# Long-convolution block with a two-layer perceptron: fixed engine order, transposing loads, and product tiles of two frequencies

## The chip, the cores and the metric

One core of one Trainium2 chip. The metric is device time in microseconds, median of several runs, lower is better. A ratio is the mean time of one kernel's fast runs over the mean of the other's fast runs of the same rounds on the same chip, so it is not quite the ratio of the two medians that are quoted beside it. The experiments ran on three chips, and the kernel before ran beside each of them (medians 287.61, 289.42 and 287.06 us): where two experiments from different chips are compared, the ratios count.

## The reference

```
x = q                                      # 2048 tokens x 512 channels, bf16
k_shift[t] = sum over j of 0..3 of shift_k[j] * k[t-j]
kv = k_shift * v
y  = irfft(rfft(kv, 4096) * rfft(ssm_k, 4096))[:2048] + kv * ssm_D      # per channel, float32
h  = x + layernorm(x) * y
out = h + relu(layernorm(h) @ w1) @ w2     # w1: 512 x 1376
```

PE is the matrix engine and PSUM the buffer that its results land in; a piece of it of 512 floats in each partition is called a bank here (pools `psF` and `psI` of the changed kernel hold eight tiles of that size). A copy out of PSUM is called an eviction. PE is called cold where its granted clock is 0.50 and warm where it is 1.00: in the kernel before, matmuls of 256 columns start 213 ns apart from 64 to 69 us, at 0.50, and 118 ns apart from 72 to 80 us, at 1.00.

Both kernels do the transforms as matrix products in two steps (64 points by 64), the filter's first and then the signal's, multiply the two spectra (the "product"), go back in two steps, and end with layer norms and the dense layers. The product stage: for each frequency column k1 PE makes the real and the imaginary part of the signal's spectrum `u` in PSUM, VectorE and GpSimd multiply them with the filter's spectrum `kf`, PE adds the four partial products into `psy`, and ScalarE copies the sum over `kf`.

## The kernel before

The parts that the change and the argument touch:

```python
# _stage2: one k1 at a time, one PSUM tile (one bank) holding both halves
for k1 in range(32):
    ps = psum.tile([P, 2, 256], F32, tag="ps", name="ps2")
    nc.tensor.matmul(out=ps[:, 0, :], lhsT=cc[:, k1, :], rhs=a_in[:, k1, :], start=True, stop=False)
    ...                                                       # four matmuls in all
    consume(k1, ps)

# product of the spectra; psum bufs=5
nc.scalar.copy(out=usb[:], in_=u[:, :, NV:DC, :])
nc.vector.tensor_tensor(out=t12v[:, :, 0:NV, :], in0=u[:, :, 0:NV, :], in1=k_same[:, :, 0:NV, :], op=ALU.mult)
nc.vector.tensor_tensor(out=t34v[:, :, 0:NV, :], in0=u[:, :, 0:NV, :], in1=k_swap(0, NV), op=ALU.mult)
... # GpSimd the last quarter of each
def finish(k1, t12, t34):
    psy = psum.tile([P, 2, DC * 64], F32, tag="psy", name="psy", bufs=3)
    ...                                                       # four matmuls, then
    nc.scalar.copy(out=kf[:, :, k1, :, :].rearrange("p r g s -> p s r g"), in_=psy[:].rearrange(...))

# first inverse: statistics of the layer norm ahead of it in VectorE's order; weights of stride 512 bytes
for t in range(NT):
    nc.vector.bn_stats(out=st1[:, t, :], in_=xh[:, t, :])
    nc.vector.bn_aggr(out=mv1[:, t, :], in_=st1[:, t, :])
for g in range(64):
    nc.tensor.matmul(out=pso, lhsT=kf[:, :, :, g, 0], rhs=dre[:], start=True, stop=False)
    nc.tensor.matmul(out=pso, lhsT=kf[:, :, :, g, 1], rhs=dim[:], start=False, stop=True)
    ...
# tail: groups of the second inverse stand between the dense layers
inv2_group(0); inv2_group(1); mlp1(0); inv2_group(2); mlp1(1); ...
```

The order of each engine's instructions was left to the scheduler.

## Time and profile before

288.3 us (median of 4 runs, 287.98 to 289.86). By stage, from busy times in stretches of the span:

| stage | us |
|---|---|
| head: tables, transposed filter | 42.5 |
| filter: first and second transform | 17.0 and 18.3 |
| signal: layout, first transform | 4.5 and 14.0 |
| product | 35.6 |
| first inverse | 36.1 |
| tail: second inverse, layer norms, dense layers | 119.4 |

The stretches themselves, the waits and the chain stand in the prediction. Two groups of the product stage are added here. The columns are line, engine, operation, output and input, shapes, count, then busy us and mean ns of one, then the idle time before it and what ended it:

```profile
L348 ACT CAST kf<-psy 128x512 fp32r<-128x512 f32 x32 | 20.1, 631 | 3.6 <-POOL t L336 1.4
L334 DVE TENSOR_TENSOR t<-ps,kf 128x384 fp32r<-128x384 f32 x32 | 17.6, 550 | 1.9 <-ACT usb L333 1.7
```

The idle time of ScalarE and VectorE ahead of these instructions is a few us of 35.6.

### The profile page before, as it was taken

To read this page: it belongs to the slowest core of one execution; us is meant where nothing else is said; L and a number is where in the kernel's file an instruction comes from. 1 tells how busy PE (TensorE), PEld (TensorE's weight loads), DVE (VectorE), ACT (ScalarE), POOL (GpSimd) and SP (SyncE) were. 2 spreads that over 40 slices of the span, in tenths; PEclk is the share of its full clock that TensorE was granted. 3 is DMA by queue.
4 is the path that set the end of the run, shared out by engine and by line. 5 is a ranking of instruction groups with operands and counts; after the bars stand their busy time and mean duration, and the time that the engine had idled before them with its cause. 6 is when DMAs were issued, how large, how long until landed. Compare 5 with 4: busy or idle time off the path is not lost.

```text
span 287.4 us, 7594 instructions
## 1 busy us (share of the span) xinstructions
PE 225.3 (78%) x3098; PEld 156.9 (55%) x3108; DVE 196.2 (68%) x449; ACT 152.9 (53%) x327; POOL 48.0 (17%) x97
## 2 busy tenths in 40 slices
PE   2027007889986699988999385999999998999994
PEld 0027005529975699977999273544544554444441
DVE  4899999985896599996836936578294258233221
ACT  1039999998885278877966313464352045113000
POOL 9921000000000389983000000000000000000000
PEclk9999555556995599996899757589999999999999
DMA  5699400000000000029156000000000200020122
GB/s 120 150 344 229 98 0 6 5 2 0 2 3 5 2 2 2 2 66 208 22 183 211 0 2 5 2 2 1 5 0 5 57 18 0 18 57 0 38 56 55
DMA packets 7876, 14.25 MB, mean 50 GB/s; under 512 B 2210, under 2 KB 5634, under 8 KB 7714
## 3 DMA queue, kind: packets, MB, share of 16 engines
q1 hardware_dynamic: 4898, 11.31, 15.5%
q10 hardware_dynamic: 2944, 2.46, 3.0%
q8 instruction: 24, 0.39, 0.6%
q14 instruction: 10, 0.08, 0.1%
HBM read 11.67 MB, written 2.10 MB: 48 GB/s over the span
## 4 chain that ended last, share of the span: by engine, by line
PE 60%; ACT 11%; DVE 9%; issue 3%; DMA 2%; ACTq 0%; DVEq 0%; SPq 0%
PE ps2m L465 12%; PE ps1m L454 12%; PE pz L422 7%; ACT a1k L270 5%; PE psi L391 4%; PE psi L392 4%; DVE st L382 3%; PE ps L112 3%; PE ps L114 3%; PE ps L115 3%; PE ps L113 3%; PE pt L444 1%; DMA xh<-in_A_q_dram 1%; ACT xfl L283 1%; DVE a1x L304 1%
## 5 line engine op out<-in xcount | busy, mean ns | idle before, releaser
L454 PE MATMUL ps1m<-hlnT,w 128*128 128x512 bf16 (+1 forms) x169 | 41.6, 387 | 2.1 <-ACT h1T L457 1.0
L465 PE MATMUL ps2m<-w,h1T 128*128 128x512 bf16 (+1 forms) x173 | 38.4, 379 | 0.2
L468 DVE TENSOR_TENSOR o<-ps2m,xh 128x512 bf16<-128x512 f32 x16 | 11.1, 692 | 29.6 <-PE ps2m L465 17.8
L391 PE MATMUL psi<-dre,kf 128*128 128x256 f32 x64 | 26.4, 412 | 5.3 <-DVE bp L396 3.1
L454 PEld LDWEIGHTS <-w 128*128 128x128 bf16 (+1 forms) x176 | 17.0, 102 | 23.2 <-issue 7.8
L457 ACT ACTIVATE h1T<-ps1m 128x512 bf16<-128x512 f32 (+1 forms) x24 | 14.4, 599 | 27.4 <-PE ps1m L454 24.7
L465 PEld LDWEIGHTS <-h1T 128*128 128x128 bf16 (+1 forms) x176 | 17.2, 98 | 20.8
L422 PE MATMUL pz<-bp,ecore 32*32 32x128 f32 x1024 | 25.2, 393 | 3.5 <-ACT zt L428 2.1
L336 POOL TENSOR_TENSOR t<-usb,kf 128x128 fp32r<-128x128 f32 x32 | 15.1, 473 | 73.3 <-ACT usb L333 71.6
L392 PE MATMUL psi<-dim,kf 128*128 128x256 f32 x64 | 25.4, 397 | 0.0
L99 PE MATMUL ps<-f_hi,kfl 32*128 32x64 bf16 x256 | 10.3, 234 | 18.5 <-ACT kfl L230 15.7
L391 PEld LDWEIGHTS psi<-dre,kf 128*128 128x128 f32 x64 | 20.0, 313 | 7.1 <-DVE bp L396 3.4
L394 ACT COPY bp<-psi 128x256 f32<-128x256 f32 x48 | 17.8, 372 | 9.3 <-PE psi L392 7.6
L428 ACT CAST zt<-pz 128x512 bf16<-128x512 f32 x16 | 8.2, 600 | 26.4 <-PE pz L422 26.4
L348 ACT CAST kf<-psy 128x512 fp32r<-128x512 f32 x32 | 20.1, 631 | 3.6 <-POOL t L336 1.4
L422 PEld LDWEIGHTS pz<-bp,ecore 32*32 32x32 f32 x1024 | 15.5, 117 | 10.4 <-issue 4.1
L392 PEld LDWEIGHTS psi<-dim,kf 128*128 128x128 f32 x64 | 20.3, 317 | 0.0
L433 DVE TENSOR_TENSOR gt<-zt,qln 128x512 bf16<-128x512 bf16 x16 | 6.5, 407 | 19.8 <-ACT zt L428 19.8
L334 DVE TENSOR_TENSOR t<-ps,kf 128x384 fp32r<-128x384 f32 x32 | 17.6, 550 | 1.9 <-ACT usb L333 1.7
L459 DVE TENSOR_SCALAR h1T<-ps1m 128x512 bf16<-128x512 f32 x20 | 13.6, 682 | 7.1 <-PE ps1m L454 7.1
L229 PE MATMUL pst<-ident,sk 128*128 128x128 bf16 x64 | 6.7, 299 | 14.0 <-DMA sk<-in_A_ssm_k_dram 14.0
L335 DVE TENSOR_TENSOR t<-ps,kf 128x384 fp32r<-128x384 f32 x32 | 17.5, 548 | 0.0
(133 smaller groups left out, 575.7 us busy)
## 6 DMA issues: line engine op xcount, KB each, us to landing
vt<-in_A_v_dram SPq DMA_DIRECT2D x16, 128.0 KB, 8.4
sk<-in_A_ssm_k_dram SPq DMA_DIRECT2D x1, 2048.0 KB
xh<-in_A_q_dram SPq DMA_DIRECT2D x4, 512.0 KB, 8.4
kh<-in_A_k_dram SPq DMA_DIRECT2D x13, 128.0 KB, 4.5
w<-in_B_w_dram SPq DMA_DIRECT2D x1, 1376.0 KB, 6.4
w<-in_B_w_dram ACTq DMA_DIRECT2D x1, 1280.0 KB, 9.6
out_dram<-o SPq DMA_DIRECT2D x32, 32.0 KB, 1.5
out_dram<-o ACTq DMA_DIRECT2D x32, 32.0 KB, 1.7
```

Of the source, the lines that this page charges most:

```text
L270: _stage1(nc, psum, kfl, f1hi, f1lo, a1k, lambda i, d, s: nc.scalar.copy(out=d, in_=s))
L334: nc.vector.tensor_tensor(out=t12v[:, :, 0:NV, :], in0=u[:, :, 0:NV, :], in1=k_same[:, :, 0:NV, :], op=ALU.mult)
L335: nc.vector.tensor_tensor(out=t34v[:, :, 0:NV, :], in0=u[:, :, 0:NV, :], in1=k_swap(0, NV), op=ALU.mult)
L336: nc.gpsimd.tensor_tensor(out=t12v[:, :, NV:DC, :], in0=usb[:], in1=k_same[:, :, NV:DC, :], op=ALU.mult)
L348: nc.scalar.copy(out=kf[:, :, k1, :, :].rearrange("p r g s -> p s r g"), in_=psy[:].rearrange("p s (r g) -> p s r g", r=DC))
L391: nc.tensor.matmul(out=pso, lhsT=kf[:, :, :, g, 0], rhs=dre[:], start=True, stop=False)
L392: nc.tensor.matmul(out=pso, lhsT=kf[:, :, :, g, 1], rhs=dim[:], start=False, stop=True)
L394: nc.scalar.copy(out=bp[:, g, :, :, :], in_=ps[:])
L422: nc.tensor.matmul(out=pz[32 * a:32 * a + 32, rg, l4, :], lhsT=ecore[rows, rho, n2, :], rhs=rhs, start=(rho == 0), stop=(rho == 1), tile_p ...
L454: nc.tensor.matmul(out=ps1[:fsz, :], lhsT=w1[:, c, fc * P:fc * P + fsz], rhs=hlnT[:, c, sc * SCW:(sc + 1) * SCW], start=(c == 0), stop=(c ...
L457: nc.scalar.activation(out=h1T[:fsz, fc, sc * SCW:(sc + 1) * SCW], in_=ps1[:fsz, :], func=ACT.Relu)
L465: nc.tensor.matmul(out=ps2[:], lhsT=h1T[:ksz, fc, t * P:(t + 1) * P], rhs=w2[:ksz, fc, :], start=(fc == 0), stop=(fc == NFC - 1))
```

## The change

Its intent: shorten the head (the shift product leaves VectorE and becomes 64 matmuls with diagonal matrices, on k and v brought in transposed by DMA; tables with fewer instructions), halve the evictions of the second transform and the multiplications of the product by taking two k1 in a tile (ScalarE keeps its 64 instructions in the product), store the product so that the first inverse loads contiguous weights, and fix the order of every engine by hand. The diff, cut to its core:

```diff
+    ctx.enter_context(tc.manual_schedule())
+    nc.sync.dma_start_transpose(out=vT[:, :, CH * c:CH * c + CH], in_=v_d[CH * c:CH * c + CH, :])
-    ... (the shift product on VectorE, 64 instructions)
+            for j in range(KS):
+                nc.tensor.matmul(out=ps[:], lhsT=wdiag[:, rg, j, :], rhs=kcs[c][:, rg, 16 - j:CH + 16 - j],
+                                 start=(j == 0), stop=(j == KS - 1))
-    psum = pl.push("psP", bufs=5, space=PSUM)
+    psum = pl.push("psP", bufs=2, space=PSUM)
+    NJ = 176
+    LAG = 2
+    def product(kp):
+        u = psum.tile([P, 2, 2, 256], F32, tag="u", name="u")
+        for s in range(2):
+            stage2(u[:, s, :, :], a1x, kp, s)
+            uj = u[:, s, :, :].rearrange("p k j -> p j k")
+            nc.scalar.copy(out=usb[:, s, :, :], in_=uj[:, po, :])
+            t = prod.tile([P, 2, 256, 2], F32R, tag=f"t{s}", name=f"t{s}")
+            ... (VectorE multiplies 176 of 256 columns from PSUM, GpSimd 80 from usb)
+    def finish():
+        psy = psum.tile([P, 2, 512], F32, tag="psy", name="psy")
+        for s, (a, b, m) in enumerate(((tr[:, 0], ti[:, 1], ineg), (tr[:, 1], ti[:, 0], ipos))):
+            for m_, t_, first in ((ipos, a, True), (m, b, False)):
+                nc.tensor.matmul(out=psy[:, s, :], lhsT=m_[:], rhs=t_.rearrange("p j k -> p (j k)"),
+                                 start=first, stop=not first)
+            nc.scalar.copy(out=kf[:, s, :, 2 * kp:2 * kp + 2], in_=psy[:, s, :].rearrange("p (j k) -> p j k", k=2))
-        nc.tensor.matmul(out=pso, lhsT=kf[:, :, :, g, 0], rhs=dre[:], start=True, stop=False)
+                nc.tensor.matmul(out=ps[:, i, :], lhsT=kf[:, c, 4 * m:4 * m + 4, :].rearrange("p r k -> p (r k)"),
+                                 rhs=d[:].rearrange("p a b -> p (a b)"), start=(c == 0), stop=(c == 1))
-    inv2_group(0)
-    inv2_group(1)
-    mlp1(0)
-    inv2_group(2)
-    ...
+    for q in range(4):
+        inv2(q)
+    gate(0, qs[0])
+    h = hln_(0)
+    transposes(0, h)
+    ...
```

A half of `u` (s = 0 or 1) is 512 floats and has a PSUM bank to itself.

## The prediction

> **What bounds the kernel now.** I read the page's forty slices first, then the chain that ended last, then cut the span where that chain changes subject and asked for busy time in each stretch. The columns are start:end, length, busy us of PE, weight loads, VectorE, ScalarE, GpSimd, granted clock, DMA share, GB/s.
>
> ```profile
> PEclk9999555556995599996899757589999999999999
> ```
>
> That row is the clock granted to PE in tenths: 5 from slice 4 to 8 (29 to 65 us), in slices 12 and 13, 23 and 25, always where PE waits for others. The stretches:
>
> ```profile
> 0.00:28.00 28.00, 8.70 (x68) 7.04 (x68) 22.68 (x58) 9.79 (x18) 16.27 (x25) 1.00 0.80 211
> 28.00:42.50 14.50, 0.00 (x0) 0.00 (x0) 14.50 (x28) 14.40 (x20) 0.00 (x0) 0.52 0.27 59
> 42.50:59.50 17.00, 13.86 (x535) 9.10 (x536) 16.96 (x30) 15.76 (x34) 0.00 (x0) 0.50 0.02 4
> 59.50:64.00 4.50, 3.20 (x46) 0.78 (x40) 3.84 (x7) 4.50 (x12) 0.00 (x0) 0.50 0.01 4
> 64.00:82.30 18.30, 18.30 (x192) 18.10 (x179) 13.46 (x32) 15.16 (x38) 0.00 (x0) 0.84 0.00 1
> 82.30:96.30 14.00, 8.24 (x485) 6.35 (x474) 10.07 (x17) 8.64 (x18) 0.00 (x0) 0.66 0.02 4
> 96.30:131.90 35.60, 33.59 (x257) 32.44 (x257) 33.64 (x72) 26.80 (x64) 30.56 (x70) 0.93 0.14 30
> 131.90:154.00 22.10, 22.07 (x97) 21.78 (x98) 10.75 (x26) 17.43 (x44) 1.19 (x2) 0.86 0.57 161
> 154.00:168.00 14.00, 9.00 (x33) 7.42 (x32) 12.55 (x39) 6.10 (x15) 0.00 (x0) 0.78 0.09 28
> 168.00:187.00 19.00, 14.90 (x529) 9.69 (x531) 9.48 (x31) 5.79 (x13) 0.00 (x0) 0.59 0.02 3
> 187.00:287.40 100.40, 93.46 (x902) 44.21 (x910) 48.27 (x117) 28.56 (x60) 0.00 (x0) 0.99 0.09 22
> ```
>
> No single engine bounds it; nine stages follow each other, each with its own limit. (1) 0 to 42.5: tables and the transposed filter. PE has nothing to do from 28 to 42.5, while VectorE (14.50 of 14.50) and ScalarE (14.40) are full. (2) 42.5 to 59.5, the filter's first transform: ScalarE, 15.76 of 17, alone carries 32 evictions at 0.49 us. (3) 59.5 to 64, layout of the signal. (4) 64 to 82.3, second transform: PE full. (5) 82.3 to 96.3, the signal's first transform: evictions on two engines, clock 0.66. (6) 96.3 to 131.9, product: PE 33.59 and VectorE 33.64 of 35.6. (7) 131.9 to 168, first inverse step: PE with slow weight loads, then a hole. (8) 168 to 187.4, second inverse and layer norms, and (9) the two dense layers, PE 93.46 of 100.4 from 187 on.
>
> Two waits name the head and the chain names the hole:
>
> ```profile
> PE ps L99 <- ACT kfl L230: 15.7, 1, 15.7
> ACT f_f L67 <- DVE f_aph L60: 15.9, 1, 15.9
> ```
> ```profile
> 154.45 1.27 DVE st L382 x2
> 155.81 0.58 DVE st L382
> ```
>
> The first transform waited 15.7 us for the filter copies on ScalarE, and that engine's sine work had itself waited 15.9 us for phase arithmetic on VectorE, which was queued among the shift products. At 154 the chain runs through sixteen layer-norm statistics on VectorE: they sit in front of an eviction that PE needs.
>
> [...]
>
> ```profile
> L391 PE MATMUL psi<-dre,kf 128*128 128x256 f32 x64 | 26.4, 412 | 5.3 <-DVE bp L396 3.1 <-ACT bp L394 1.4 <-ACT kf L348 0.8
> L391 PEld LDWEIGHTS psi<-dre,kf 128*128 128x128 f32 x64 | 20.0, 313 | 7.1 <-DVE bp L396 3.4 <-ACT bp L394 2.7 <-ACT kf L348 1.0
> L113 PEld LDWEIGHTS ps<-a1x,c2s 128*128 128x128 f32 x32 | 6.6, 207 | 0.0
> L345 PEld LDWEIGHTS psy<-t,ineg 128*128 128x128 f32 x32 | 6.1, 192 | 0.0
> ```
>
> The inverse's stationary tile has a 512-byte stride and loads in 313 ns, so its matmuls start 225 ns apart at full clock; contiguous tiles load in 192 to 207 ns (cold ones included) and start 118 apart. [...] In the changed program's built order [...] each of its 16 blocks waits for the eviction of the block before, though that lies in other columns. [...]
>
> **The change part by part**, as estimates from rows above and from single durations in the groups by shape.
>
> Head. Removed: the 64 instructions of the shift product on VectorE (8 chunks of 8, about 0.6 us each, 40 us), the cos/sin phase pairs, the quarter-size sine calls, three 3.5 us table clears. The filter load goes first: here it took 8.8 us from issue to use, so it is there at about 9.5. 64 transposes took 6.74 us: PE ends at 16.2. ScalarE: sine over 32 elements took 229 ns and over 512 took 633, so 0.84 ns an element; four of 2048 cost 7.7 us, starting when VectorE's turns are done (two of about 1.25 us after a 2 us GpSimd iota, so about 7), so to 14.7; then three copies of 1.03. Five more go to VectorE. The copies end at about 18 instead of 42.5.
>
> First transforms. 32 evictions split evenly: VectorE 16 x 0.62 = 9.9, plus a first batch of 0.9 and issue gaps: the signal's stage already does this and took 14.0, with 3 us of PE gaps. Four row groups now alternate before the second weight comes, so I take 12.5 each (were 17.0 and 14.0).
>
> Second transform of the filter: 128 matmuls x 118 ns = 15.1, plus a cold start of some 3: 18 (was 18.3). Evictions, half as many and twice as wide, stay under it.
>
> Signal side. The shift product was hidden on VectorE in the head; now it is 64 diagonal matmuls x 216 ns (the dense layers' spacing) = 13.8 plus a last multiply of 1: 15. Chunks 2 and 3 of k reuse the buffer of the filter's transform, so their load is issued only when that ends; PE has 6.9 us of chunks 0 and 1 meanwhile[...]. Then 64 transposes 6.8 plus the last copy 1.2: 8. Together 23 where 4.5 stood.
>
> Product: PE 16 x (8 x 118 ns + 4 x 225) = 29.5; ScalarE 16 x 2 x (0.29 + 0.63) = 29; VectorE 32 x (550 ns + 320 x 1.04 - 90 of overlap) = 25; GpSimd 32 parts of 320 elements: 128 take 0.42 us start to start, so between 0.8 and 1.05, 26 to 34. VectorE is relieved, the others not: with fill and drain 35 (was 35.6).
>
> First inverse: 128 x 118 ns = 15.1; ScalarE 20 x 0.53 + 8 x 0.6 = 15.4; VectorE 12 x 0.64 + 16 x 0.42 = 14.4. All even: 17 (was 36.1). The statistics leave this stage.
>
> To here 18 + 12.5 + 18 + 15 + 8 + 12.5 + 35 + 17 = 136, against 168: 32 gained.
>
> Tail (was 119.4). The fourth group of 256 second-inverse records ran 228.1 to 232.5, 17.3 ns each at full clock; the first ran 23 ns each, half cold. A block is 64 records: 1.1 to 1.5, plus 0.35 for the last one's own duration, 0.6 for the ScalarE copy, 0.1 between: 2.1 to 2.5, and 16 strictly in turn are 34 to 40: 36. Before, groups 3 and 4 took 5.0 and 4.4 beside other work. After the last copy: square root 0.3, reciprocal 0.2, normalise 0.4, four rounds of transposes and copy through one PSUM buffer at 1.3: 6. Dense layers 352 x 216 ns = 76, cold start 2. The three later transpose groups stand in line in front of matmuls, 4 x (0.4 + 0.65) less the last: 11. Two square roots stand in ScalarE's queue ahead of the relus and wait for statistics: 2 x 2 = 4. End: last sum 0.7, four stores issued and landed 3.3: 4. Sum 36 + 6 + 76 + 2 + 11 + 4 + 4 = 139, so 20 lost.
>
> 136 + 139 = **275 us**, 13 less than before.
>
> **Rivals.** (a) The tail loses nothing: if block waits were hidden and the transposes short, the tail would stay near 119 and the time about 255. For it: one fixed order saves end-of-kernel store waits (11.8 us of waits for stores, mostly slack). Against: the waits stand in the built order. (b) The tail eats all: the half-idle second inverse keeps PE cold (stage 5 cooled to 0.50 under such a duty), 40 us for it, and cold dense matmuls after each transposes round; with 4 more in each of the two first transforms, 290. (c) A transfer becomes the bound: [...] 5 to 10 us on the path, 283. (d) GpSimd, at 8-byte runs 128 bytes apart, [...] 42 us of product, 282.
>
> **Range and chances.** The head and the first inverse are worth some 43 us and rest on measured rows; the conv stage costs 18 with little doubt. The tail is the weak term, 125 to 148, and loads and GpSimd can only add. 258 to 291 should hold it. Below 282.6 counts as over 2% faster: 0.72. Within 2%: 0.21. Slower: 0.07.
>
> **What would show it right or wrong.** Right: first matmul of the first transform near 18; weight loads of the first inverse near 190 ns and its stage 16 to 18; no statistics in front of its evictions; 16 waits of the second inverse for its ScalarE copy, about 0.7 each; PE idle on the transposes' copy in three places. Wrong: a wait on the k transposing loads, a product over 39, or a second inverse of 20 us, which would make the whole about 258.

What was cut from the prediction, at the marks, came from elsewhere or was assumed, and no trace of this case shows it: rules on the clock, on memory access and on waits in PSUM, the rate of transposing loads and what was concluded from it, the rate that rival (c) assumed and the time of an instruction that rival (d) assumed. The sentence on the 16 blocks speaks of the second inverse; that the loads of k would be hidden behind 6.9 us of work is an assumption (in the run no matmul waited for them). Three figures of the product's term come from the kernel before: 1.04 ns an element is the slope between VectorE's 425 ns for 256 elements and 692 for 512, the 90 ns are two instructions of 550 ns that start 460 apart, and 216 ns is the spacing of the dense layers' matmuls of 512 columns. The 225 ns for 512 columns in the product were an estimate and no row of that trace; the kernel with both tiles split later gave 230.

## The result

347.97 us (median of 4 runs, 346.56 to 348.56) against 288.28: ratio 1.2056, 95% interval 1.201 to 1.210. **Slower by 21%**, where 275 us were predicted. The result is correct in value.

The clock row of the forty slices, which answers to the first line that the prediction shows:

```profile
PEclk9955899985555555555555995555589999999999
```

In slices 10 to 21 (counted from 0), that is from about 87 to 187 us, PE never leaves half clock. The stretches of the changed kernel (same columns as in the prediction: start:end, length, busy us of PE, weight loads, VectorE, ScalarE, GpSimd, then clock, DMA share, GB/s):

```profile
0.00:18.10 18.10, 6.63 (x64) 6.50 (x64) 16.11 (x31) 12.83 (x10) 10.29 (x18) 0.98 0.99 231
18.10:33.10 15.00, 9.13 (x512) 7.73 (x512) 9.66 (x18) 8.51 (x17) 11.63 (x16) 0.50 0.46 81
...
51.00:65.70 14.70, 13.88 (x64) 6.14 (x64) 11.43 (x17) 0.60 (x1) 0.00 (x0) 1.00 0.48 75
65.70:73.10 7.40, 5.97 (x66) 5.87 (x67) 4.91 (x5) 4.06 (x4) 0.00 (x0) 1.00 0.00 0
73.10:87.20 14.10, 8.67 (x513) 7.24 (x513) 9.94 (x16) 8.21 (x16) 0.79 (x2) 0.58 0.02 5
87.20:187.30 100.10, 66.79 (x192) 46.95 (x192) 28.49 (x32) 28.57 (x64) 28.71 (x36) 0.50 0.00 0
187.30:205.60 18.30, 17.36 (x128) 17.16 (x128) 16.09 (x31) 15.22 (x29) 2.85 (x5) 0.89 0.98 268
205.60:241.00 35.40, 24.29 (x1024) 15.04 (x1024) 9.16 (x28) 10.44 (x18) 0.00 (x0) 0.54 0.02 5
```

| stage | before | predicted | measured |
|---|---|---|---|
| head | 42.5 | 18 | 18.1 |
| filter, first transform | 17.0 | 12.5 | 15.0 |
| filter, second transform | 18.3 | 18 | 17.9 |
| signal: diagonal matmuls; transposes | 4.5 | 15; 8 | 14.7; 7.4 |
| signal, first transform | 14.0 | 12.5 | 14.1 |
| **product** | 35.6 | **35** | **100.1** |
| first inverse, to the first block of the second | 36.1 | 17 | 18.3 |
| tail | 119.4 | 139 | 139.2 |

One stage carries the miss: 65 of the 73 us. In it PE, VectorE, ScalarE and GpSimd are busy 66.8, 28.5, 28.6 and 28.7 of 100.1 us, and the 66.8 are at half clock. Apart from PE's, the single instructions have about the sizes that were predicted (VectorE 892 ns where the prediction's sum gives 793, GpSimd 886, ScalarE 292 and 601), so none of them is slow; they stand one after another. The waits say what for (us in total, times, longest):

```profile
PE u L232 <- DVE t L322: 21.7, 16, 1.4
PE psy L332 <- ACT kf L334: 10.9, 16, 0.7
```

One wait of each kind in each of the 16 pairs. The timeline shows a full pair, from 139.96 to 146.16 us; columns are start, length, engine, instruction, count, and in brackets the idle time before it and its releaser (only some lines are copied):

```profile
139.96 0.58 PE L232 MATMUL u<-a1x,c2n 128*128 128x256 f32 x1 [1.36 <-DVE t L322]
...
142.08 0.60 ACT L334 CAST kf<-psy 128x512 fp32r<-128x512 f32 x1 [0.56 <-PE psy L332]
142.73 1.22 PE L332 MATMUL psy<-t,ipos 128*128 128x512 f32 x2 [0.69 <-ACT kf L334]
143.75 0.41 PE L232 MATMUL u<-a1x,c2c 128*128 128x256 f32 x1
...
144.89 0.29 ACT L318 COPY usb<-u 128x160 f32<-128x160 f32 x1 [0.30 <-PE u L234]
145.22 0.89 DVE L322 TENSOR_TENSOR t<-u,kf 128x704 fp32r<-128x704 f32 x1 [2.71 <-ACT usb L318]
...
146.16 0.58 PE L232 MATMUL u<-a1x,c2n 128*128 128x256 f32 x1 [1.36 <-DVE t L322]
```

PE writes the first half of `u` (143.75), ScalarE copies its part (144.89), VectorE multiplies (145.22), and only then PE starts the second half (146.16), which needs none of that. The same happens in `psy`: its second half waits for the copy of the first. 16 x 6.20 us = 99.2. By the trace, which infers releasers from semaphore events, these two matmuls wait for a reader of the other half. The reading that the experiments test is that dependencies are kept by PSUM tile, and both halves belong to one tile. In the timeline no later matmul starts inside the gaps of 0.69 and 1.36 us, so whatever was ready behind such a wait stood too.

### The profile page after: what moved, and what is told of

Read it like the earlier page. It is cut to its first block, busy times and chain, and to the rows that moved or that the text cites. A ratio compares the mean times of both kernels' runs of the same rounds, so it can differ in the third digit from the quotient of the medians.

```text
span 344.8 us, 7155 instructions
## 1 busy us (share of the span) xinstructions
PE 254.9 (74%) x3094; PEld 169.8 (49%) x3104; DVE 163.0 (47%) x313; ACT 135.0 (39%) x240; POOL 54.3 (16%) x75
## 4 chain that ended last, share of the span: by engine, by line
PE 66%; ACT 10%; DVE 10%; issue 3%; ACTq 0%; DVEq 0%
PE ps2m L495 11%; PE ps1m L482 10%; PE psy L332 10%; PE pz L420 7%; PE u L232 6%; PE psi L393 5%; DVE t L322 5%; PE pkv L282 4%; PE u L234 4%; ACT kf L334 3%; ACT zt L423 3%; PE ps2k L232 3%; PE ps2k L234 2%; ACT hlnT L470 2%; DVE st L433 2%
## 5 line engine op out<-in xcount | busy, mean ns | idle before, releaser
L322 DVE TENSOR_TENSOR t<-u,kf 128x704 fp32r<-128x704 f32 x32 | 28.5, 892 | 64.2 <-ACT usb L318 64.1
L322 POOL TENSOR_TENSOR t<-usb,kf 128x320 fp32r<-128x320 f32 x32 | 28.3, 886 | 65.0 <-ACT usb L318 64.9
L332 PE MATMUL psy<-t,ipos 128*128 128x512 f32 x48 | 29.2, 684 | 10.9 <-ACT kf L334 10.9
L484 ACT ACTIVATE h1T<-ps1m 128x512 bf16<-128x512 f32 (+1 forms) x44 | 25.8, 595 | 18.0 <-PE ps1m L482 17.7
L232 PE MATMUL u<-a1x,c2n 128*128 128x256 f32 x32 | 16.0, 499 | 21.7 <-DVE t L322 21.7
L318 ACT COPY usb<-u 128x160 f32<-128x160 f32 x32 | 9.3, 292 | 42.8 <-PE u L234 42.8
L332 PEld LDWEIGHTS psy<-t,ipos 128*128 128x128 f32 x48 | 13.3, 318 | 22.7 <-ACT kf L334 22.5
L232 PEld LDWEIGHTS u<-a1x,c2n 128*128 128x128 f32 x32 | 10.0, 311 | 26.4 <-DVE t L322 26.4
L433 DVE BATCH_NORM_STATS2 st<-xh 128x6 f32<-128x512 bf16 x32 | 19.7, 678 | 0.0
L470 ACT COPY hlnT<-pt 128x512 bf16<-128x512 bf16 x16 | 9.4, 585 | 20.2 <-PE pt L469 20.2
L393 PE MATMUL psi<-dim,kf 128*128 128x256 f32 x64 | 16.9, 301 | 0.0
```

Source lines behind the costliest of these rows:

```text
L232: nc.tensor.matmul(out=ps[:, kk, :], lhsT=w_re[:, k1, :], rhs=a_in[:, k1, :], start=True, stop=False, skip_group_check=True)
L322: eng.tensor_tensor(out=t[:, :, j, :], in0=in0.unsqueeze(1).to_broadcast([P, 2, n, 2]), in1=kfr[:, :, j, ks], op=ALU.mult)
L332: nc.tensor.matmul(out=psy[:, s, :], lhsT=m_[:], rhs=t_.rearrange("p j k -> p (j k)"), start=first, stop=not first)
L393: nc.tensor.matmul(out=ps[:, i, :], lhsT=kf[:, c, 4 * m:4 * m + 4, :].rearrange("p r k -> p (r k)"), rhs=d[:].rearrange("p a b -> p (a b)" ...
L433: nc.vector.bn_stats(out=st[:, i, :], in_=xh[:, 4 * q + i, :])
L484: nc.scalar.activation(out=h1T[:fsz, fc, :], in_=ps1[:fsz, :], func=ACT.Relu)
```

## The experiments

The theory, A: **a wait by whole PSUM tile, at the head of an in-order queue**, makes PE, ScalarE and VectorE take turns; the half clock follows from it. Rivals: B, the engines' instructions bound the stage; C, PE enters the stage cold and cannot warm up; E, two halves in one tile are slow in themselves. All twelve kernels gave correct values. Product stage below means first `u` matmul to first `psi` matmul (`psi` is the first inverse's PSUM tile); tail means first `pz` matmul (second inverse) to the end of the span.

### Both tiles split

```diff
-        u = psum.tile([P, 2, 2, 256], F32, tag="u", name="u")
+            u = psum.tile([P, 2, 256], F32, tag=f"u{s}", name=f"u{s}")
-        psy = psum.tile([P, 2, 512], F32, tag="psy", name="psy")
+            psy = psum.tile([P, 512], F32, tag=f"psy{s}", name=f"psy{s}")
```

> The changed kernel, except that in the product stage each half of u and of psy is a PSUM tile of its own (four tags, two buffers of 512 floats each); banks, buffers, instructions and their sizes are the same. Theory A (the second half's matmuls wait for readers of the first half, because both lie in one PSUM tile): the product stage falls from 100.3 us to 35-40, its granted clock rises from 0.50 to over 0.8, the wait of u for the VectorE product disappears, and the whole is 282 to 290 us. Rival B (GpSimd at 886 ns or VectorE at 892 ns an instruction, or 8-byte accesses, bound the stage): no change, 345 to 350. Rival C (the PE comes to the stage at a clock of 0.58 and cannot warm up): the waits go but the clock stays at 0.50; 16 x (8 x 215 + 4 x 430) ns = 55 us, whole about 303.

Measured: 277.53 us, ratio to the kernel before 0.9645 (0.962 to 0.967). The stretch of its product stage:

```profile
85.80:119.20 33.40, 32.59 (x192) 29.38 (x192) 27.10 (x33) 26.30 (x64) 29.17 (x36) 0.93 0.00 1
```

33.4 us for 100.1, the clock at 0.93, PE busy 32.59 of 33.40, and neither of the two waits is left on PE. A pair takes 1.88 us, its PE time at full clock. Same instructions, same sizes, same bytes of PSUM, a correct result: the waits protected nothing. Theory A holds; B and C fall, since the engines were not the limit and PE came in as cold (0.52 in the stage before) and warmed up. Stage and total came out below what was expected before the run (35 to 40, and 282 to 290 us). The total is 2.5 us from the predicted 275.

### One tile split at a time

> Only u's halves are separate tiles; psy stays one tile. Theory A: the chain of a pair becomes eight matmuls, two of psy, the copy of psy's first half (0.6 us and two hand-overs), two of psy: 2.7 us at full clock to 4.9 at half clock, so a stage of 45 to 80 us and a whole of 293 to 328. Theory A also says that neither half of the repair alone gets the whole gain. Rival B: no change.

> Only psy's halves are separate tiles; u stays one tile. Theory A: the chain of a pair becomes four matmuls, copy 0.3, VectorE 0.9, four matmuls and four of psy: 3.2 us at full clock to 5.6 at half clock, so a stage of 51 to 90 us and a whole of 298 to 338. The first matmul of u's second half still waits for VectorE. Rival B: no change.

Measured: with `u` alone split 294.07 us (ratio 1.023, 1.020 to 1.025), product stage 48.5 us; with `psy` alone split 306.97 us (1.068, 1.065 to 1.072), 63.0 us. The first fence has the wait that is left and the stage of the kernel with `u` split, the second those of the kernel with `psy` split:

```profile
PE psy L332 <- ACT kf L334: 11.0, 16, 0.7
86.70:135.20 48.50, 36.78 (x193) 28.07 (x193) 27.05 (x32) 27.32 (x64) 28.54 (x36) 0.95 0.00 1
```
```profile
PE u L232 <- DVE t L322: 22.0, 16, 1.4
87.20:150.20 63.00, 39.98 (x192) 32.71 (x192) 28.66 (x33) 26.29 (x64) 29.39 (x37) 0.85 0.00 1
```

Each split removes exactly its own wait and leaves the other, to a tenth of a us or three. The two repairs save 51.6 and 37.1 us alone and 66.7 together: less than the sum, because each alone already lets PE warm up. The clocks of 0.95 and 0.85 are means: both stages begin at half clock, and PE is at full clock from 4.7 us into the first and from 19 us into the second, with the gaps of the wait that is left still in every pair.

### The waits kept, PE kept busy

```diff
+            if s == 1:
+                filler(5)                      # matmuls into a spare bank that nobody reads
             stage2(u[:, s, :, :], a1x, kp, s)
-        psy = psum.tile([P, 2, 512], F32, tag="psy", name="psy")
+        psy = psum.tile([P, 2, 512], F32, tag="psy", name="psy", bufs=1)
+            if s == 1:
+                filler(3)                      # ahead of psy's second half
```

> The changed kernel with both shared tiles and all its waits, but matmuls that nobody reads stand in the two stalls: five of 512 columns in front of u's second half, three in front of psy's second half, into a spare bank (psy keeps one buffer instead of two, which no wait of the pair uses). It separates the waits from the cold clock. If half clock is a consequence of the stalls and doubles their price: the clock rises to over 0.9, a pair takes 4.3-5.1 us instead of 6.2, the stage 70-82, the whole 318-330; so of the 67 us between the changed kernel and e1 some 20-30 are clock and 37-47 are waits. If the stalls alone are the cost: 98-104 us, 346-352. If PE stays at half clock: the fillers outlast the stalls by 1.3 us a pair, 120 us, 368.

Measured: 321.43 us (ratio 1.117, 1.112 to 1.123). The stage:

```profile
86.60:163.50 76.90, 71.21 (x320) 50.77 (x320) 28.41 (x32) 28.18 (x64) 29.45 (x36) 0.96 0.00 1
```

With useless matmuls in the stalls the clock is 0.96 and the stage 76.9 us, in the middle of what was expected. So of the 66.7 us about 23 are the half clock that the stalls bring (100.1 - 76.9) and about 43 the stalls themselves (76.9 - 33.4).

### The tile kept, the order changed

```diff
+        product(kp, 0)                         # first half of pair n+1 ...
+        if kp >= 1:
+            product(kp - 1, 1)                 # ... ahead of the second half of pair n
```

> As e3 (psy in two tiles, u left as one tile of both halves), but the program order is changed: the first half of pair n+1 is put in front of the second half of pair n, so the wait by whole tile stays in the program and something else stands in front of it. Theory A' (the cost is the wait standing at the head of an in-order queue, not the shared tile): product 63.0 us of e3 falls to 38-46, the whole from 307.0 to 283-291. Not as low as e1 (33.4), because the first half of pair n+2 waits for VectorE's readers of the second half of pair n, just issued. Rival E (two halves in one tile are slow in themselves[...]): it stays at 60-65 us and 305-309.

Only `u` is shared here, as `psy` is split. Measured: 296.04 us (ratio 1.024, 1.020 to 1.027), product stage 49.6 us. The direction is A's, the size is missed by 4 us and E is not needed: with the same shared `u` the stage takes 63.0 us in one order and 49.6 in another. What I had not counted is that both halves reach ScalarE late, back to back, so a pair takes 2.91 us and PE still waits 0.76 us in each.

Then one line was taken out of the changed kernel, so that the scheduler orders the engines again:

```diff
-    ctx.enter_context(tc.manual_schedule())
```

> The changed kernel with one line taken out, the one that keeps the order of the program; the scheduler orders the engines again, as in the kernel before, and the shared tiles stay. The built order then takes the first halves of two pairs in front of their second halves. By the theory (shared tile plus fixed order make the stall): the product falls from 100 us to 42-58 without any change of tiles, the tail moves by a few us either way, and the whole is 288-308. If sharing alone does it: 345 and over.

> e1 (both tiles split) with the scheduler ordering the engines. What the hand-made order itself is worth once the tiles are split: product and head as in e1 within 3 us; in the tail the scheduler's order puts half of the second inverse between transposes and dense matmuls, so some of the 20 us lost in the tail comes back: 262-273 (e1 277.5). If the hand order is better than the scheduler's: 278 and over.

Measured, with shared tiles: 272.59 us (ratio 0.949, 0.943 to 0.955); its stage:

```profile
88.20:128.60 40.40, 37.86 (x192) 29.30 (x192) 28.46 (x32) 26.57 (x64) 29.52 (x35) 0.93 0.00 1
```

With split tiles: 265.31 us (0.923, 0.918 to 0.927), product stage 34.0. I expected 288 to 308 for the first and was too pessimistic: the scheduler takes the first halves of two pairs before their second halves and sets `psy` matmuls between, and the shared tiles then cost 40.4 - 34.0 = 6.4 us instead of 66.7. So the loss is neither the shared tile nor the fixed order by itself: it needs both. The tail is 124.7 us in both, against 139.0 in the hand order.

### The tail

The prediction gave back 20 us in the tail. Four kernels ask what of it was necessary. First, in the changed kernel, two PSUM tiles taken in turn for the second inverse:

```diff
-    pz = psum.tile([P, 4, 4, P], F32, name="pz", bufs=1)
+            pz = psz.tile([P, 4, 512], F32, tag="pz", name="pz")          # bufs=2, eight banks
```

> The changed kernel, except that the second inverse's blocks alternate between two PSUM tiles of four banks each (the pool of the dense layers is opened after it); the product is left as it is. If the tail's 36 us of second inverse are the 16 waits for the copy of the block before, as predicted: a block falls from 2.20 us to 1.1-1.3 and the stage from 36 to 18-22 us, the whole by 14 to 18, to 330-334. If the block is bound by PE (1.54 us busy each at half clock) and the clock does not rise, the stage falls only to 25 and the whole by 11, to 337.

Measured: 339.84 us, 7 to 8 less than the changed kernel, with the tail at 132.6 us instead of 139.2. **A miss** (330 to 334 were expected): the wait went, and after the first five blocks a block still took 1.7 to 2.0 us. Two lines of PE's timeline:

```profile
218.68 2.79 PE L420 MATMUL pz<-bp,ecore 32*32 32x128 f32 x128 [0.68 <-issue]
222.41 2.78 PE L420 MATMUL pz<-bp,ecore 32*32 32x128 f32 x128 [0.94 <-issue]
```

After each run of 128 small matmuls PE stands for 0.6 to 1.3 us with no releaser in the trace ("issue"); the waits had hidden this. The DMA records of the same trace point to a cause that I had overlooked. The queue of instruction transfers (packets, MB, share of the 16 engines' span):

```profile
q8 instruction: 24, 0.39, 0.5%
```

Its packets are of 16 KB, one comes for each such run (128 matmuls and their 128 weight loads), and each of the six runs that follow a gap starts 1.2 to 1.5 us after one has landed (at 217.26 and 220.95 us for the two lines above; read from the packed trace). My reading is that PE waits for its own instructions; no run tests it. The same kind of gap, 8.5 us in 7 places, six of them with a packet landing 1.2 to 1.5 us before their end, lies in the two first transforms of the changed kernel, which have 512 such small matmuls each and came out 2.5 and 1.6 us above the prediction.

Then, from the kernel with both tiles split, transposes one at a time between output tiles of the second dense layer:

> e1, and the later three groups of transposes are not issued four in a row but one (the last two) between output tiles of the second dense layer, so the copy out of the single PSUM buffer runs beside matmuls. The prediction put these groups at 11 us; PE waits 8.1 us for the copy in 12 waits, of which 3 belong to the first group, which stays. Expected: the wait falls to about 3.5 us and the whole from 277.5 to 271-275. If ScalarE's relus in front of the copy, or the buffer, only move the wait: within 1.5 us of 277.5.

Measured: 273.43 us (ratio 0.944, 0.940 to 0.949), 4.1 less by the medians and some 5.8 by the ratios (another chip), as expected; PE's wait for the transposes' copy falls from 8.1 us in 12 waits to 4.0 in 6.

And the blocks of the second inverse between dense matmuls:

> e1 (both tiles split), and the order of the tail is changed by hand: the second inverse's groups 2 and 3 are put block by block between groups of dense matmuls, transposes go one token tile at a time, layer norms earlier. If the tail's loss against the kernel before (139.8 against 119.4) is the second inverse standing alone, cold and waiting block by block: 8 of 16 blocks fall from 2.2 us to 1.1-1.3, 8 us, the chain between inverse and dense layers partly hides, 5 us, the transposes 5 us: the whole falls from 277.5 to 256-264. If the loss lies in the dense layers (their 96 us), it stays within 3 us of 277.5.

Measured: 261.20 us (0.904, 0.900 to 0.908), as expected; the tail 121.6 us. In the timeline a block between dense matmuls passes in 1.4 to 1.9 us (I had expected 1.1 to 1.3) where one alone takes 2.2, and no gap of PE around it is over 0.33 us. The last step fills the first four transposes as well:

```diff
-    transposes(0, hl[0])
+    for i in range(4):
+        transposes(0, hl[0], [i])
+        inv2(2, [i])
```

> e6 (261.2) with the third group of the second inverse put between the first four transposes, whose copies leave PE waiting some 0.65 us each, and the fourth group into the first dense layer's first strip. Expected: 2-4 us less, 257-259.5; if ScalarE, which makes both copies, is the bound there, no change.

Measured: 256.37 us (0.892, 0.887 to 0.897), 4.8 less by the medians; but the two ran on different chips, and by the ratios (0.904 and 0.892 of about 288 us) it is some 3.4, inside the expected 2 to 4. This version is faster than both kernels: 11% below the kernel before. Its stages, product, first inverse, tail:

```profile
87.90:121.80 33.90, 33.04 (x193) 29.80 (x193) 27.17 (x33) 26.24 (x64) 29.14 (x37) 0.91 0.00 1
121.80:138.70 16.90, 15.95 (x128) 15.48 (x128) 15.83 (x31) 15.18 (x29) 2.70 (x4) 1.00 1.00 273
138.70:255.90 117.20, 104.07 (x1429) 52.48 (x1440) 54.65 (x151) 46.91 (x85) 0.00 (x0) 0.91 0.08 22
```

The tail is 117.2, below the 119.4 of before.

### One part alone on the kernel before

The statistics' hole in the first inverse was counted as a gain of its own, so it was closed in the kernel before: the sixteen `bn_stats` and `bn_aggr` are written after the loop of the first inverse.

> The kernel before, with one part of the change alone: the sixteen layer-norm statistics are written after the first inverse's evictions instead of in front of them. If the hole at 154 to 168 us is VectorE's statistics in front of an eviction: PE's 11 us gap goes, the statistics (12 us of VectorE) then stand beside the second inverse and hold up its gating by 2-5 us; whole 278-283 (from 287.6). If the hole was the weight loads or the kf writes: 286-289.

Measured: 286.41 us (ratio 0.990, 0.985 to 0.995). **A miss** of the first expectation (278 to 283) and inside the second, the weight loads (286 to 289). The stages tell why:

```profile
131.50:162.40 30.90, 30.16 (x131) 29.03 (x132) 15.68 (x40) 22.48 (x57) 1.19 (x2) 0.94 0.45 127
162.40:285.00 122.60, 108.88 (x1430) 54.32 (x1440) 65.91 (x173) 35.15 (x74) 0.00 (x0) 0.92 0.08 19
```

The hole is gone and the stage is 30.9 us instead of 36.1, no less, because PE then runs through at the 225 ns of the strided weights in the kernel before (128 x 225 = 28.8). The tail grows by 3.2, to where the statistics moved. The hole was real and worth some 3 us by itself (0.5 to 1.5% by the interval); most of the 18 to 19 us that the changed kernel gains in this stage go with the contiguous weights (192 ns a load there by the median, 313 to 317 by the mean in the kernel before) and the wider evictions, which no run separates. In the kernel with split tiles the stage takes 16.9 us.

## Why the prediction was wrong

**The failed step is the term "Product", put at 35 us**, "with fill and drain", from PE 29.5, ScalarE 29, VectorE 25 and GpSimd 26 to 34. Those four sums were right or nearly (measured busy: 28.6, 28.5 and 28.7 on the last three, so VectorE 14% over its 25; PE 32.6 in the split kernel, where its clock is up). Wrong was the step from them to 35: a stage is as long as its fullest engine only where the engines may run at the same time, and that was taken over from the kernel before without looking at the waits of the new program. It measured 100.1, as a chain of 6.2 us in each pair. The case is plain because I had read a wait of this kind, for a reader of other columns, in the second inverse of the same built program, and priced it there (2.1 to 2.5 us a block; 2.2 measured), and did not ask where else one tile has two halves. The two are not quite alike: blocks of the second inverse share their banks, while the halves of `u` lie in different ones. That the wait in `u` protected nothing was shown (33.4 us of product and correct values without it); for the wait between blocks that share a bank it was not. None of the four rivals was it; rival (d), GpSimd's access pattern, looked at the same stage for the wrong reason: GpSimd took 0.886 us an instruction and was busy for 28.7 us, not 42.

**Point by point.** *Head 18*: 18.1. *Second transform of the filter 18*: 17.9. *Signal side 23*: 22.1, and no wait on the transposing loads, so rival (c) fell. *First transforms 12.5 each*: 15.0 and 14.1; the step from the wider order of row groups to 12.5 failed by 4 us in all; the two stages hold 8.5 us of gaps whose cause no run tests. *First inverse 17*: 16.9 to 18.3; its share of the hole was over-told, as the run on the kernel before shows. *Tail 139*: 139.2, so rivals (a) and (b) fell for the changed kernel; in the last tail kernel, with the product repaired, half of the blocks among transposes and dense matmuls, the tail is 117.2 and the time 256.4, near the 119 and 255 that (a) gave for such a case. With the product stage repaired by the split alone the kernel is at 277.5, inside the range and 2.5 from the number. The other terms held within 2.5 us each; that the total is so near is in part luck, since the repaired product (33.4 for 35) makes up for some of the first transforms.

## What to carry to other kernels

When a change packs two independent pieces of work into one PSUM tile, look in the built order for a matmul that waits for a reader of the other piece; if each piece has readers of its own and the order is fixed, give each piece a tile of its own, which costs no memory. Adding up busy time per engine gives the length of a stage only after the waits of the new program have been read through; one pair written out in order of time, as in the timeline above, would have shown about 4.5 us at full clock, by my estimate (4.8 a pair with the fillers), and 6.2 at half clock instead of 2. A scheduler that looks ahead may hide such a wait (6 us here) that a hand-made order lays bare (67 us), and the small matmuls of the second inverse were better put between large ones: standing alone they ran at a clock of 0.50 (from 210 to 241 us of the changed kernel) and a block took 2.2 us, between dense matmuls 1.4 to 1.9 us.

## What the runs show of the hardware

- Waits in PSUM: two halves in different banks ran without a wait between them and gave correct values (33.4 us of product); no run leaves out a wait within one bank. The changed program waits across two banks, by whole tile, and here this cost 66.7 us.
- Gaps and the clock: gaps of 1.4 us in every pair did not cool PE in the kernel with `psy` split, once it was warm, but gaps no longer than that went with a PE that stayed cold. In the changed kernel PE came to the product at 0.50, its busy stretches between gaps of 0.69 and 1.36 us were 2.1 us long, and it stayed at 0.50 for 100 us. With these gaps filled it reached full clock (0.96 over the stage), and also with `psy` split, from 19 us into the stage on; there two of the busy stretches join into one, about 4 us by my estimate from the 2.1.
- Instructions: with two `pz` tiles PE stood for 0.6 to 1.3 us after each run of 128 small matmuls (32 by 32 by 128 columns) with their 128 weight loads, each time until 1.2 to 1.5 us after a packet of 16 KB of the instruction queue had landed. That it waits for the packet is my reading and not shown.
- Transposing loads: from 9.4 to 24.0 us, when nearly only those of k and v were moving, the changed kernel's DMA carried 209 GB/s; they were hidden.
